# An attention kernel with scaled fp16 weight halves: other steps for the scales' transposes and for loading and splitting one weight, a later low part, another load priority

## The chip, the cores and the metric

The kernel runs on one core of one Trainium2 chip. The core has five engines with instruction queues of their own: PE (TensorE, matmuls into PSUM), DVE (VectorE), ACT (ScalarE), POOL (GpSimd) and SP (SyncE, which here issues all DMAs). Each queue is worked off in order; engines wait for one another by semaphores. The metric is the device time of one execution in microseconds (us), as the median of several runs. A difference under about 0.5% can't be told from no change.

## The reference

Two layers of attention (A) and gated MLP (B) alternate, A B A B, over x of 2048 rows by 640, with the same weights in both layers. Cut to what matters:

```python
def _A_ref(x, wq, wk, wv, wo, beta):        # H = 32 heads of Dh = 20; N = 4 segments of L = 512
    q, k, v = heads(x @ wq), heads(x @ wk), heads(x @ wv)
    for s in range(N):
        logits = einsum("bhqd,bhkd->bhqk", qs, ks) * scale + mask
        a_dot = einsum("bhqk,bhkd->bhqd", softmax(logits), vs)
        a_mem = einsum("bhld,bhde->bhle", phi(qs), M) / (phi(qs) . z + 1e-6)
        outs.append(g * a_mem + (1 - g) * a_dot)
        M, z = M + phi(ks)^T vs, z + sum(phi(ks))
    return concat(outs) @ wo

def _B_ref(x, w_in, w_sp, b_sp, w_out):
    z = gelu(x @ w_in); z1, z2 = halves(z); z2 = layernorm(z2)
    return (z1 * (w_sp @ z2 + b_sp)) @ w_out

x = x + _A_ref(layernorm(x), ...);  x = x + _B_ref(layernorm(x), ...)     # twice
```

## The kernel before, in words

Every matmul operand is kept as two fp16 parts, high and low, whose sum has nearly fp32 precision; a product of two such operands is three fp16 products. A weight is first scaled by a power of two. ACT then writes its high part (`split_scaled`, L81), and DVE subtracts to get the low part (L82). The scales come from the largest entry: DVE reduces the weight's pieces (`other_scales`, L268), PE transposes the row maxima (`pow2_parts`, L60, tile `wtp`), DVE takes the maximum and writes a small diagonal (L62, L64, `wmx` and `wdg`), PE spreads it over all partitions (L67, `wbc`), and DVE makes the power of two of it and its inverse (L69 to L74, `pw` and `iv`).

A layer has three phases: 1a (attention, class `Attention`), 1b (`phase1b`, the rest of the output projection and the first MLP product) and 2 (`phase2`). Phase 1a goes by steps t = -16 to 164, with 16 pairs of heads in each of 4 segments, 64 pairs in all; five steps make a group that serves two pairs. In a step PE does score products for the maxima (`by_queries`, into PSUM tile `mp`, reduced by DVE to `mxs`, L1310 and L1313) and for the exponentials (`by_keys`, into `es`; ACT writes their exponentials `P`, L1287). Once in a group (`maxes`) PE transposes the maxima (`mtp`), ACT and DVE write them in two parts (`mr`, L1333 and L1335), and four DMAs put them beside the keys. `cast` splits P into `PH` (ACT, L1322) and `PL` (POOL, or DVE for the last pair's second head, L1324), `pvs` multiplies them with the values (`pv`), and `combine` normalises the result on DVE (L1364 to L1374 with a `TENSOR_REDUCE` at L1371) or with POOL's help. Only one `pv` tile exists, so the next pair's products wait until `combine` has read it.

Between these products PE does dense ones: the projections of q and k (`unit`, `qps` and `kps`), of values (`value`, `vps`) and of the output (`project`, `yps`). These share two PSUM buffers. `out` of a key unit ends with ACT's exponential of `kps` (L1137) and DVE's `relu` (L1142), after which the buffer is free. The memory part has `read` (`num`, drained by `gm`, L1188) and `update` (`mup`, drained by `mst`, L1209). The tiles `num`, `mup`, `mtp`, `wtp` and `wbc` all have the tag "ms" and share a **single PSUM buffer**: each waits until the one ahead has been drained.

In the first layer weights have to be made as well. `background` does this between the steps: pieces of all four remaining weights are loaded and reduced from step 5 on, then come the scales' transposes (steps 39 and 40), then the rows of w_o are loaded into five buffers of their own (steps 45.5 to 47.5) and split (steps 48 to 53), and then w_in's second half, `wi1`, is loaded and split two pieces behind (from step 57 on, ten pieces). In the second layer all parts are only loaded.

PE's order is that of the program (`manual_schedule`). On the other engines a scheduler sets the order from priorities and a model of the times: `high_priority(offset=n)` lets instructions go ahead by n, and `issue_after(e)` keeps instructions of the block behind e on e's engine, without a wait. `behind(engine)` does the latter for the step's own exponentials (ACT) or maxima (DVE). `post(k, f)` runs f k steps later.

Of the kernel before, what the change touches and what calls it, by code (L numbers as in the profile page):

```python
# [8 lines left out]
F32 = mybir.dt.float32  # L9
# [5 lines left out]
ALU = mybir.AluOpType  # L15
# [3 lines left out]
S, D, H, DH, NSEG = 2048, 640, 32, 20, 4  # L19
L = S // NSEG  # L20
NT = S // 128
KD = D // 128
F, FH = 1728, 864
FHH = FH // 2
# [10 lines left out]
HP2 = 300  # L35
# [226 lines left out]
def other_scales(g, place, pool, psum, tag):  # L262

    nc = g.nc
    raw = []

    def largest():
        nc.vector.tensor_reduce(*raw.pop(0), AX.X, ALU.max, apply_absolute_value=True)  # L268

    for i, w in enumerate((g.wo, *g.wi, g.wu)):  # L270
        width = D if w.cols == D else w.cols // 2
        j = 0
        for k in range(w.nk):
            n = min(128, w.dram.shape[0] - 128 * k)
            for c in range(0, w.cols, width):
                t = place(width)[:n, :width]
                nc.sync.dma_start(t, w.dram[k * 128:k * 128 + n, w.c0 + c:w.c0 + c + width])
                raw.append((g.wap[:n, i, j:j + 1], t))
                if len(raw) > 2:
                    largest()  # L280
                yield True
                j += 1
    while raw:
        largest()
        yield True
    nc.vector.tensor_reduce(g.wam[:, 3:7], g.wap, AX.X, ALU.max)
    yield False
    parts = pow2_parts(g, pool, psum, tag, g.wam, 3, 4)
    next(parts)
    yield False  # L290
    next(parts)
    nc.vector.tensor_scalar(g.yw, g.pw[:, 0:1], g.pw[:, 3:4], 2.0 ** -19, ALU.mult, ALU.mult)
    nc.vector.tensor_scalar(g.sc[:, 8:10], g.pw[:, 4:6], 2.0 ** -24, None, ALU.mult)
# [44 lines left out]
def phase1b(g, o_d, x, x1_d, z1_d, zh, zl):  # L338

    nc, tc = g.nc, g.tc  # L340
    with ExitStack() as ctx:
# [14 lines left out]
        def load(t):  # L356
            if t < NWO:
                x1 = pe2.tile([128, D], F32, tag="x1", name="x1")
                g.loaded[t] = nc.sync.dma_start(x1, x1_d[t])
                return (x1,)  # L360
            xt = px2.tile([128, D], F32, tag="xt", name="xt")
            with tc.issue_after(g.loaded[ORDER[ORDER.index(t) - 1]].ins):
                g.loaded[t] = nc.sync.dma_start(xt, x[t])
            o = px1.tile([128, 2, KD, 128], F16, tag="o", name="o")
            d = o_d[t // 4][(t % 4) * 128:(t % 4 + 1) * 128]
            nc.sync.dma_start(o.rearrange("p i k c -> p (i k) c"), d.rearrange("p i c -> p (i c)"), transpose=True)
            return xt, o[:, 0], o[:, 1]
# [78 lines left out]
        def z1_half(t, zp):  # L446
            z1 = p2.tile([128, FH], F32, tag="z1", name="z1")
            nc.scalar.activation(z1.rearrange("p (n c) -> p n c", n=2), zp[:, :, :FHH], AF.Gelu_apprx_tanh, scale=g.zi[0])  # L448
            nc.sync.dma_start(z1_d[t], z1)

        with tc.high_priority(offset=HP2):
            a = load(0)
            xn = attn_out(0, *a)
            a = load(ORDER[1])
            th = xn_t(*xn)
        for i, t in enumerate(ORDER):
# [6 lines left out]
            if i + 2 < NT:  # L463
                a = load(ORDER[i + 2])
# [449 lines left out]
DVE, ACT = mybir.EngineType.DVE, mybir.EngineType.Activation  # L914


class Attention:
# [68 lines left out]
    def place(self, width):  # L986

        i = self.turn
        self.turn = (i + 1) % (3 if width == D else 4)
        if i < 2:  # L990
            return self.bg.tile([128, D], F32, tag="bg", name="wst")
        if i == 2:
            self.spare = self.pad.tile([128, 2 * FHH], F32, tag="pad", name="wst")
            return self.spare
        return self.spare[:, FHH:]
# [320 lines left out]
    def cast(self, n, h):  # L1316

        nc = self.nc
        P = self.pair(n)
        PH = self.pl3.tile([128, 1280], F16, tag="PH", name="PH")  # L1320
        PL = self.pl2.tile([128, 1280], F16, tag="PL", name="PL")
        nc.scalar.copy(PH, P[:, h])  # L1322
        for c in (slice(0, 640), slice(640, 1280))[::-1 if n % 2 and h else 1]:
            (nc.gpsimd if h == 0 or n < self.N - self.TAIL else nc.vector).tensor_tensor(PL[:, c], P[:, h, c], PH[:, c], ALU.subtract)  # L1324
        self.P[n, h] = (PH, PL)

    def maxes(self, d):
# [69 lines left out]
    def run(self, nseg=NSEG):  # L1397
# [51 lines left out]
        for s in range(nseg):  # L1449
# [4 lines left out]
            for c in seq:  # L1454
                beg = G * s - LEAD + span * acc / tot
                if c == "v":
                    t, w = next(vt), V
# [3 lines left out]
                    it = self.value(t)  # L1461
                    assert s == 0 or beg > G * s + 3, (s, t, beg)
                elif c == "p":
                    t, w = next(pt), Y
                    ev.append((beg - 3, 1, t))
                    it = self.project(t)
                    assert beg - 3 > G * (t // 4 + 1) + 6, (s, t, beg)
                else:
                    m, w = int(c), U
                    if m == 0 and s == nseg - 1:  # L1470
                        continue
                    it = self.unit(s + (m == 0), m)
# [17 lines left out]
        def background():  # L1490

            g = self.g
            made = g.wo.made
            yield 5
            if not made:
                for i, _ in enumerate(other_scales(g, self.place, self.pl1, self.pm, "ms")):
                    yield 5 + i
            yield 45
            yield 45.5
            for j, (w, width) in enumerate(((g.wo, D), (g.wi[1], FHH))):  # L1500
                w.tiles(g.top[j])
                if made:
                    it = w.load(self.bg, width, "bg")
                    times = [46 + 8 * j + 1.4 * i for i in range(99)]
                elif j:
                    it = w.behind(self.place, width, 2)
                    times = [56 + 1.9 * i for i in range(99)]
                else:
                    parts = [g.top[1].tile([128, 2160], F32, tag=f"wi1{x}", name=f"wst{x}3")[:, :3 * D].rearrange("p (k c) -> p k c", c=D) for x in "hl"]
                    rows = iter([parts[k // 3][:, k % 3] for k in range(KD)])  # L1510
                    it = w.behind(lambda _: next(rows), width, KD)
                    times = [46 + i / 2 for i in range(KD)] + [49 + 1.4 * i for i in range(99)]
                for i in range(99):
                    with self.tc.issue_after(self.fetched.ins):
                        if next(it, it) is it:
                            break
                    yield times[i]
            if not made:
                for i, (nm, x, k) in enumerate((nm, x, k) for nm in "qk" for x in range(2) for k in range(KD)):
                    yield 70 + 2 * i  # L1520
                    with self.tc.issue_after(self.fetched.ins):
                        self.nc.sync.dma_start(g.wqk[nm + "hl"[x]][:, k], g.w[nm][x][:, k])

        for _ in early():
            pass
        streams = [[next(it), i, it] for i, it in enumerate((fills(), background(), dense(), reads()))]

        def until(t):
# [8 lines left out]
        for t in range(-LEAD, END):  # L1537
            self.now = t
            d, i = divmod(t + self.LF + 5 + self.DM, 5)
            if i in (0, 2) and 0 <= 2 * d < N:  # L1540
                self.fetch(2 * d + i // 2)
            d, i = divmod(t - 7, 5)
            if i in (0, 2) and 0 <= 2 * d < N:
                p = 2 * d + i // 2
# [6 lines left out]
            d, i = divmod(t + self.DM, 5)  # L1551
# [5 lines left out]
            for d, i, o in PVS:  # L1557
                if t % 5 == i % 5 and 0 <= 2 * (t // 5 - i // 5) < N:
                    p = 2 * (t // 5 - i // 5) + d
# [93 lines left out]
```

## Time and profile before

| | us |
|---|---|
| median of 3 runs | 2235.47 |
| lowest and highest | 2233.04 and 2241.97 |
| the profiled execution | 2232.87 |
| its span, first to last instruction | 2231.2 |
| DVE busy | 1624.2 (73%) |
| POOL busy | 1404.3 (63%) |
| ACT busy | 1252.3 (56%) |

The span is what the profiler saw between the first and the last instruction; all times in views of the trace are counted from its start. Phase 1a of the first layer lies at about 40 to 605 us and that of the second at about 1160 to 1697 us. A view of waits gives the time that an engine stood idle before a line, and the instruction that ended the idle time; when several were waited for it names the last.

### The profile page before, as it was taken

Reading aid. Unit: us, or ns where it says so; the run is one execution under the profiler, and the core shown is the slowest. Engines: PE = TensorE matmul, PEld = TensorE weight load, DVE = VectorE, ACT = ScalarE, POOL = GpSimd, SP = SyncE. Lnnn points to the kernel's source line nnn. Section 1 sums busy time; section 2 is a strip of 40 time slices with the busy share of each in tenths; the row PEclk is TensorE's granted clock in tenths of the full one; section 3 lists DMA queues with packets and bytes.
Section 4 is the critical chain, followed back from the end, with each engine's and each line's share of the span. In section 5 each row is a group of like instructions: output and inputs, shape, how many; then the busy total and the mean of one; then the engine's idle time right before and its main releaser. Section 6 shows DMA issues by size and latency. Waiting matters only on the chain.

```text
span 2231.2 us, 53044 instructions
## 1 busy us (share of the span) xinstructions
PE 2092.0 (94%) x21322; PEld 1264.7 (57%) x21322; DVE 1624.2 (73%) x2889; ACT 1252.3 (56%) x1641; POOL 1404.3 (63%) x1172
## 2 busy tenths in 40 slices
PE   6898788999899999999998999989999999999999
PEld 3554555666555555555554556656675555555555
DVE  8788778788677758888746787787875765676563
ACT  4587688788644433333325887878884433333331
POOL 3387888888645446466513888988895533564660
PEclk9999899999999999999999999999999999999999
DMA  6665556444676686676455356552456345877752
GB/s 185 157 177 141 157 150 188 109 120 126 166 195 188 180 260 191 155 189 175 132 170 129 98 128 166 127 129 75 125 137 152 98 123 175 216 181 177 166 150 83
DMA packets 537703, 342.79 MB, mean 154 GB/s; under 512 B 411600, under 2 KB 463312, under 8 KB 537456
## 3 DMA queue, kind: packets, MB, share of 16 engines
q1 hardware_dynamic: 537456, 339.39, 56.8%
q8 instruction: 167, 2.74, 0.5%
q14 instruction: 80, 0.66, 0.1%
HBM read 159.18 MB, written 92.55 MB: 113 GB/s over the span
## 4 chain that ended last, share of the span: by engine, by line
PE 67%; DVE 14%; ACT 7%; DMA 5%; issue 4%; POOL 2%; SPq 1%; DVEq 0%; ACTq 0%; POOLq 0%
PE zp L412 12%; PE ga L669 12%; PE cyp L705 7%; PE pv L1353 4%; PE qps L1110 3%; PE mp L1249 3%; PE gb L669 3%; PE vps L1051 3%; PE yps L1083 3%; PE gc L669 3%; PE gd L669 3%; DVE mxs L1313 3%; PE kps L1110 2%; PE es L1249 2%; ACT PH L1322 2%
## 5 line engine op out<-in xcount | busy, mean ns | idle before, releaser
L1324 POOL TENSOR_TENSOR PL<-P,PH 128x640 f16<-128x640 f32 x384 | 539.4, 1433 | 91.8 <-PE pv L1353 74.2
L1313 DVE TENSOR_REDUCE mxs<-mp 128x2 f32<-128x1024 f32 (+2 forms) x384 | 320.6, 862 | 135.3 <-PE mp L1240 133.7
L1287 ACT ACTIVATE P<-es,sc 128x1024 f32<-128x1024 f32 (+1 forms) x256 | 271.3, 1060 | 97.0 <-PE es L1240 92.3
L639 POOL TENSOR_TENSOR ts<-ts,wt 128x512 f32<-128x512 f32 x196 | 281.8, 1449 | 11.0
L412 PEld LDWEIGHTS <-th 128*128 128x128 f16 x1920 | 188.0, 98 | 169.3 <-issue 6.6
L1322 ACT CAST PH<-P 128x1280 f16<-128x1280 f32 x192 | 239.6, 1248 | 2.5 <-PE pv L1353 1.0
L669 PEld LDWEIGHTS <-wts 128*128 128x128 f16 x1536 | 150.7, 98 | 134.6 <-issue 6.7
L669 PE MATMUL ga<-zh,wts 128*128 128x432 f16 x768 | 212.0, 348 | 3.9 <-ACT u L736 3.9
L308 POOL TENSOR_TENSOR lnrs<-lnve,mhalf 128x1 f32<-128x1 f32 x96 | 59.7, 629 | 230.0 <-DVE lnve L307 223.7
L1324 POOL TENSOR_TENSOR PL<-Pb,PH 128x640 f16<-128x640 f32 x124 | 176.8, 1454 | 19.8 <-PE pv L1353 18.6
L412 PE MATMUL zp<-wi,th 128*128 128x432 f16 x960 | 181.2, 346 | 3.6 <-ACT z L448 3.6
L1051 PE MATMUL vps<-wvh,xt 128*128 128x320 f16 x640 | 155.5, 309 | 30.3 <-DVE relu L1142 22.1
L639 POOL TENSOR_TENSOR ts<-wt,wt 128x512 f32<-128x512 f16 x28 | 34.4, 1230 | 227.7 <-DMA wt<-wn 227.7
L669 PEld LDWEIGHTS <-wt 128*128 128x128 f16 x1152 | 112.7, 98 | 96.5
L1353 PE MATMUL pv<-vs,PH 128*128 128x41 f16 x2560 | 159.5, 183 | 8.2 <-DVE gm L1374 5.9
L705 PE MATMUL cyp<-wuh,ut 128*128 128x320 f16 (+1 forms) x896 | 163.6, 299 | 2.6 <-DMA ut<-un 1.8
L705 PEld LDWEIGHTS <-ut 128*128 128x128 f16 (+1 forms) x1344 | 131.1, 98 | 57.4 <-DMA ut<-un 3.9
L1249 PEld LDWEIGHTS <-qk 64*128 64x128 f16 (+1 forms) x2048 | 77.6, 94 | 149.4 <-issue 130.9
L1353 PE MATMUL pv<-vs,PL 128*128 128x41 f16 x2560 | 157.2, 182 | 2.2 <-POOL PL L1324 2.2
L412 PE MATMUL zp<-wi1h,th 128*128 128x432 f16 x640 | 149.8, 349 | 1.9 <-DMA th<-xnhl 1.9
L1353 PEld LDWEIGHTS <-PH 128*128 128x128 f16 x2560 | 139.4, 96 | 15.8 <-issue 5.9
L523 DVE SCALAR_TENSOR_TENSOR wn<-wr,wsc,wn 128x512 f16<-128x512 f32 x126 | 92.2, 770 | 75.5 <-ACT wn L522 75.4
(224 smaller groups left out, 5283.3 us busy)
## 6 DMA issues: line engine op xcount, KB each, us to landing
qk<-st SPq DMA_DIRECT2D x256, 120.0 KB
wr<-in_B_w_sp_dram SPq DMA_DIRECT2D x60, 512.0 KB
z<-z SPq DMA_DIRECT2D x32, 432.0 KB
cz<-z SPq DMA_DIRECT2D x32, 432.0 KB
xt<-in_A_x_dram SPq DMA_DIRECT2D x32, 320.0 KB
st<-qhl SPq DMA_DIRECT2D x40, 256.0 KB
st<-khl SPq DMA_DIRECT2D x40, 256.0 KB
x<-x SPq DMA_DIRECT2D x32, 320.0 KB
```

The source lines that it names most:

```text
L412: nc.tensor.matmul(zp[:, n, :FHH], a[:, k, :], b[:, k, c:c + FHH], start=(k == 0 and j == 0), stop=(k == KD - 1 and j == 2))
L639: nc.gpsimd.tensor_tensor(t, a, t if b == "t" else get(b), ALU.add if op == "+" else ALU.subtract)
L669: nc.tensor.matmul(ps, w[:, a, k % 4, :], z[:, k, j, :], start=start and k == 0 and i == 0, stop=k == NP - 1 and i == 2, skip_group_check= ...
L705: nc.tensor.matmul(yp[:, n, :320], a[:kn[k], k, :], b[:kn[k], k, n * 320:(n + 1) * 320], start=(k == 0 and j == 0), stop=(k == KO - 1 and ...
L1051: nc.tensor.matmul(ps, a[:, k, c], b[:, k, n * 320:(n + 1) * 320], start=(i == 0), stop=(i == 14))
L1110: nc.tensor.matmul(ps, a[:, k, c], b[:, k, :], start=(i == 0), stop=(i == 14))
L1249: nc.tensor.matmul(out[:, h, o:o + w], a[r, ac], b[r, bc], start=o == 0, stop=False, skip_group_check=True)
L1287: g.exp = nc.scalar.activation(P, E, AF.Exp, scale=g.esc)
L1313: e = nc.vector.tensor_reduce(mx[:, :, n, j], mp[:, :, o:o + w], AX.X, ALU.max)
L1322: nc.scalar.copy(PH, P[:, h])
L1324: (nc.gpsimd if h == 0 or n < self.N - self.TAIL else nc.vector).tensor_tensor(PL[:, c], P[:, h, c], PH[:, c], ALU.subtract)
L1353: nc.tensor.matmul(pv[:, i, h, :41], x[:, c:c + 128], v[:, j, h0 + h, :], start=(j == 0 and x is PH), stop=(j == i and x is PL), skip_grou ...
```

## The change

There are four edits.

1. `background`, first layer: the scales' transposes go from step 39 to step 41, and the second part (the spreading matmul and the powers of two) from step 40 to step 45. The five row loads of w_o go from steps 45.5 to 47.5 to steps 42 to 44, between the two parts. The splits go from steps 48 to 53.2 to steps 47 to 52.6.
2. All loads and splits of `background` are put behind the step's exponentials on ACT.
3. `cast`: the low part that DVE makes for the last pair is posted two steps later, behind that step's combination.
4. `phase1b`: the load of the first row gets a priority offset of 900 in place of 300.

```diff
-        with tc.high_priority(offset=HP2):
-            a = load(0)
+        with tc.high_priority(offset=3 * HP2):
+            a = load(0)
+        with tc.high_priority(offset=HP2):
             xn = attn_out(0, *a)
...
+        def low(engine):
+            for c in (slice(0, 640), slice(640, 1280))[::-1 if n % 2 and h else 1]:
+                engine.tensor_tensor(PL[:, c], P[:, h, c], PH[:, c], ALU.subtract)
+
+        if h == 0 or n < self.N - self.TAIL:
+            low(nc.gpsimd)
+        else:
+            self.post(2, lambda: low(nc.vector))
...
-                for i, _ in enumerate(other_scales(g, self.place, self.pl1, self.pm, "ms")):
+                scales = other_scales(g, self.place, self.pl1, self.pm, "ms")
+                for i, more in enumerate(scales):
+                    if not more:
+                        break
                     yield 5 + i
+                yield 41
+                next(scales)
...
+            def steps(it, times):
+                for t in times:
+                    with self.tc.issue_after(self.fetched.ins), self.behind(ACT):
+                        if next(it, it) is it:
+                            break
+                    yield t
...
+                it = g.wo.behind(lambda _: next(rows), D, KD)
+                yield 42
+                yield from steps(it, [42.5, 43, 43.5, 44, 45])
+                next(scales, None)
+                yield 47
+                yield from steps(it, [48.4 + 1.4 * i for i in range(99)])
+                g.wi[1].tiles(g.top[1])
+                yield from steps(g.wi[1].behind(self.place, FHH, 2), [56 + 1.9 * i for i in range(99)])
```

The first place is the transpose of the scales in the first layer. On PE it stood before the change behind a step's score products and ahead of a query projection:

```order
L1240 LDWEIGHTS stepk
L1240 MATMUL es<-eye,stepk 128x64
L60 MATMUL wtp<-ident,wam 4x128
L1110 LDWEIGHTS wqh
L1110 MATMUL qps<-xt_302,wqh 128x512
```

Now it stands behind a pair's value products, ahead of the last seven products of the key projection (line numbers from 449 on are shifted):

```order
L1361 LDWEIGHTS PL
L1361 MATMUL pv<-vs_297,PL 128x41
L60 MATMUL wtp<-ident,wam 4x128
L1111 LDWEIGHTS wkh
L1111 MATMUL kps<-xt_302,wkh 128x512
```

The transpose has moved two steps on, past a `num`. On DVE the two operations that follow it stood ahead of `relu`, and the powers of two right behind `gm`:

```order
L1209 TENSOR_TENSOR mst_305<-mup,bmask 128x168
L306 BN_AGGR lnmv<-lnst 128x2
L307 TENSOR_SCALAR lnve<-lnmv 128x1
L62 TENSOR_REDUCE wmx<-wtp 4x1
L64 TENSOR_SCALAR wdg<-ident,wmx 4x4
L1142 SCALAR_TENSOR_TENSOR relu<-kps,relu 128x512
L1313 TENSOR_REDUCE mxs_304<-mp 128x2
L1148 SCALAR_TENSOR_TENSOR phl<-relu,sc,phl 128x512
L1184 SCALAR_TENSOR_TENSOR den<-num,sc,gate 128x24
L1187 RECIPROCAL den<-den 128x24
L1188 TENSOR_TENSOR gm<-num,den 128x4x120
L69 COPY pw<-wbc 128x4
```

Now the same engine reaches `wmx` only after `gm` and three more operations:

```order
L1189 TENSOR_TENSOR gm<-num,den 128x4x120
L1033 TENSOR_SCALAR xt<-xt,lnmv,lnrs 128x640
L1372 TENSOR_TENSOR rs<-pv,iomg 128x8
L1129 SCALAR_TENSOR_TENSOR qhl<-qps,qhl 128x512
L62 TENSOR_REDUCE wmx<-wtp 4x1
L1373 RECIPROCAL rs<-rs 128x8
L64 TENSOR_SCALAR wdg<-ident,wmx 4x4
L1385 TENSOR_TENSOR ab<-pv,rs 128x328
L1141 SCALAR_TENSOR_TENSOR phq<-qps,relu 128x512
L1314 TENSOR_REDUCE mxs_303<-mp 128x2
```

The pair `wmx`, `wdg` has moved behind `gm`, and `relu` no longer has them ahead of it. The second place is the splitting of w_o's rows on ACT (`woh`). Before the change the five stood together, the first of them ahead of the key unit's exponential:

```order
L1287 ACTIVATE P<-es,sc 128x2x512
L81 ACTIVATE woh<-wsth_4007,iv 128x640
L320 CAST xnhl<-xt 128x640
L1322 CAST PH<-P 128x1280
L1056 ACTIVATE vs_297<-vps 128x16x20
L1389 CAST ohl<-gm 128x640
L1137 ACTIVATE kps<-kps,sc 128x512
L81 ACTIVATE woh<-wsth_4007,iv 128x640 x2
L81 ACTIVATE woh<-wstl_4008,iv 128x640
L1147 ACTIVATE phl<-relu,sc 128x512
L81 ACTIVATE woh<-wstl_4008,iv 128x640
```

Now none stands in that stretch; the first comes a group later, behind two exponentials and ahead of ACT's half of `mr`:

```order
L1288 ACTIVATE P<-es,sc 128x2x256
L1288 ACTIVATE Pb<-es,sc 128x2x256
L81 ACTIVATE woh<-wsth_3705,iv 128x640
L1341 ACTIVATE mr<-mtp 16x128
L1323 CAST PH<-P 128x1280
L320 CAST xnhl<-xt 128x640
L1057 ACTIVATE vs_297<-vps 128x16x20
L1288 ACTIVATE Pb<-es,sc 128x2x512
L81 ACTIVATE woh<-wsth_3705,iv 128x640
```

The splits have spread, each behind an exponential; those of `wi1` have moved in the same way, one or two places back. The third place is the end of phase 1a in the first layer, on DVE. Before, the last low part stood ahead of the combination's reduction:

```order
L1364 TENSOR_TENSOR rs<-pv,iomg 128x8
L1365 RECIPROCAL rs<-rs 128x8
L1324 TENSOR_TENSOR PL<-Pb,PH 128x640 x2
L1371 TENSOR_REDUCE pv<-pv 128x160
L1089 SCALAR_TENSOR_TENSOR xt<-yps,sc,xt 128x320
L1373 TENSOR_TENSOR pv<-pv,rs 128x4x2x20
```

Now it stands behind the reduction, and still ahead of the combination's other two operations:

```order
L1372 TENSOR_TENSOR rs<-pv,iomg 128x8
L1373 RECIPROCAL rs<-rs 128x8
L1379 TENSOR_REDUCE pv<-pv 128x160
L1327 TENSOR_TENSOR PL<-Pb,PH 128x640 x2
L1090 SCALAR_TENSOR_TENSOR xt<-yps,sc,xt 128x320
L1381 TENSOR_TENSOR pv<-pv,rs 128x4x2x20
```

One operation has changed places with it. In the second layer it already stood so, and no instruction of any engine changes its place there. The load of the first row of phase 1b stands at the same place in SP's queue before and after, in both layers.

More of the change, by code (lines that the diff above doesn't have):

```diff
@@ L1322, in cast @@
         nc.scalar.copy(PH, P[:, h])
-        for c in (slice(0, 640), slice(640, 1280))[::-1 if n % 2 and h else 1]:
-            (nc.gpsimd if h == 0 or n < self.N - self.TAIL else nc.vector).tensor_tensor(PL[:, c], P[:, h, c], PH[:, c], ALU.subtract)
+        def low(engine):
[5 more added lines that the diff above has]
+            self.post(2, lambda: low(nc.vector))
         self.P[n, h] = (PH, PL)
@@ L1495, in background @@
             if not made:
-                for i, _ in enumerate(other_scales(g, self.place, self.pl1, self.pm, "ms")):
+                scales = other_scales(g, self.place, self.pl1, self.pm, "ms")
+                for i, more in enumerate(scales):
+                    if not more:
+                        break
                     yield 5 + i
[L1498 to L1514, printed above, removed]
@@ L1515, in background @@
+                yield 41
[3 more added lines that the diff above has]
+                    with self.tc.issue_after(self.fetched.ins), self.behind(ACT):
                         if next(it, it) is it:
                             break
-                    yield times[i]
+                    yield t
+            g.wo.tiles(g.top[0])
+            if made:
+                yield 45.5
+                yield from steps(g.wo.load(self.bg, D, "bg"), [46 + 1.4 * i for i in range(99)])
+                g.wi[1].tiles(g.top[1])
+                yield from steps(g.wi[1].load(self.bg, FHH, "bg"), [54 + 1.4 * i for i in range(99)])
+            else:
+                parts = [g.top[1].tile([128, 2160], F32, tag=f"wi1{x}", name=f"wst{x}3")[:, :3 * D].rearrange("p (k c) -> p k c", c=D) for x in "hl"]
+                rows = iter([parts[k // 3][:, k % 3] for k in range(KD)])
+                it = g.wo.behind(lambda _: next(rows), D, KD)
[4 more added lines that the diff above has]
+                yield from steps(it, [48.4 + 1.4 * i for i in range(99)])
+                g.wi[1].tiles(g.top[1])
+                yield from steps(g.wi[1].behind(self.place, FHH, 2), [56 + 1.9 * i for i in range(99)])
```

## The prediction

> **What bounds the kernel now.** The page comes first:
>
> ```profile
> span 2231.2 us, 53044 instructions
> PE 2092.0 (94%) x21322; PEld 1264.7 (57%) x21322; DVE 1624.2 (73%) x2889; ACT 1252.3 (56%) x1641; POOL 1404.3 (63%) x1172
> ```
>
> PE is busy nearly throughout and its order is fixed, so what the change can win is time in which PE stands still; what it adds beside PE costs nothing until PE waits for it. The edits move instructions in the first layer only, which gives a control: the second layer runs the same PE program in phase 1a without scales and splits. So the second view is a table of windows of both layers, cut at the start of ACT's `mr` (L1333), which comes once in a group. The first row goes from the 9th `mr` of a layer to the 10th, the next two are one group each, the fourth covers five; four rows are of the first layer, four of the second.
>
> ```profile
> core 0: us, PE busy (x) PEld busy (x) DVE busy (x) ACT busy (x) POOL busy (x), PEclk, DMA share, GB/s
> 197.17:222.50 25.33, 17.71 (x241) 11.11 (x239) 19.20 (x45) 15.37 (x20) 16.12 (x15) 0.93 0.33 89
> 222.50:247.25 24.75, 15.91 (x235) 10.28 (x233) 15.02 (x30) 18.11 (x26) 17.84 (x16) 0.79 0.71 184
> 247.25:266.04 18.79, 17.59 (x258) 12.72 (x255) 16.26 (x26) 11.81 (x16) 17.34 (x15) 0.91 0.40 113
> 266.04:352.10 86.06, 74.86 (x1151) 48.04 (x1150) 67.26 (x117) 70.17 (x90) 72.41 (x67) 1.00 0.58 158
> 1313.33:1332.22 18.89, 16.60 (x248) 10.35 (x241) 16.05 (x30) 15.46 (x21) 16.37 (x15) 1.00 0.46 112
> 1332.22:1349.24 17.02, 14.29 (x228) 9.69 (x221) 14.90 (x30) 14.43 (x20) 16.24 (x16) 0.90 0.90 214
> 1349.24:1368.46 19.22, 17.76 (x258) 12.58 (x255) 11.70 (x23) 11.81 (x15) 16.16 (x16) 0.91 0.69 167
> 1368.46:1444.81 76.35, 73.88 (x1151) 47.41 (x1150) 55.40 (x105) 65.04 (x80) 69.73 (x66) 1.00 0.53 132
> ```
>
> The first layer takes longer by 25.33 - 18.89 = 6.4, by 24.75 - 17.02 = 7.7, by -0.4 and by 86.06 - 76.35 = 9.7 us: 23.4 us in all. That is the cost of making weights in this stretch, and a ceiling for the change. Third, PE's waits over these windows, first layer, then second:
>
> ```profile
> PE vps L1051 <- DVE relu L1142: 8.8, 1, 8.8
> PE es L1249 <- ACT P L1287: 3.9, 5, 1.6
> PE wbc L67 <- DVE gm L1188: 3.5, 1, 3.5
> PE es L1249 <- ACT Pb L1287: 1.8, 2, 1.4
> ...
> PE vps L1051 <- DVE relu L1142: 2.7, 1, 2.7
> PE es L1249 <- ACT P L1287: 1.2, 2, 1.0
> ```
>
> The extra time is mostly named here: one wait of 8.8 us against 2.7, one of 3.5 us for the scales' second matmul, and 5.7 us for exponentials against 1.2.
>
> **The scales' transposes (first window).** Two waits belong to them, the 3.5 us above and this one:
>
> ```profile
> 207.13 0.27 PE L60 MATMUL wtp<-ident,wam 128*4 128x128 f32 x1 [2.70 <-DVE lnmv L306]
> 207.75 0.72 DVE L64 TENSOR_SCALAR wdg<-ident,wmx 4x4 f32<-4x4 f32 x1
> ```
>
> Both are waits for the one "ms" buffer: `wtp` needs `mup` drained (`mst` stands just ahead of the named `lnmv` on DVE), `wbc` needs `num` drained by `gm`. Their removal brings the window to the control's 18.89, but `wtp` comes back between `gm` and `mtp`. The control and the stretch behind the old `wbc` price that:
>
> ```profile
> 1328.50 0.65 DVE L1188 TENSOR_TENSOR gm<-num,den 128x480 f32<-128x480 f32 x1
> 1329.45 0.39 PE L1331 MATMUL mtp<-ident,mxs 128*16 128x128 f32 x2
> ...
> 219.06 0.38 PE L1110 MATMUL kps<-xt,wkh 128*128 128x512 f16 x1
> 221.38 0.39 PE L1331 MATMUL mtp<-ident,mxs 128*16 128x128 f32 x2
> ```
>
> In the control `gm` ends at 1329.15 and `mtp` follows at 1329.45, with the seven `kps` products and a step's scores done ahead. With `wtp` placed ahead of these, they wait for `gm` too: 0.27 us for `wtp`, then 221.38 - 219.06 = 2.3 us until `mtp`, so 1329.15 + 2.6 = 1331.75, which is **2.3 us late**. DVE's `wmx` comes after three operations and is drained in that time. Bounds: 0.3 us (only `wtp` itself), and 3.3 us (`wmx` and `wdg`, about 1.0 us, also delay `ab` behind them, for which `pv` waits). I take 2.3, since the order on PE forces it. Term: 6.4 - 2.3 = **4.1 us** gained (3.1 to 6.1).
>
> **The loads of w_o and their first split (second window).** ACT, in order of time:
>
> ```profile
> 227.82 1.11 ACT L1287 ACTIVATE P<-es,sc 128x1024 f32<-128x1024 f32 x1 [0.69 <-PE es L1240]
> 233.06 0.83 ACT L81 ACTIVATE woh<-wsth,iv 128x640 f16<-128x640 f32 x1 [4.13 <-DMA wsth<-in_A_wo_dram]
> 233.79 0.71 ACT L320 CAST xnhl<-xt 128x640 f16<-128x640 f32 x1
> 236.51 0.66 ACT L1137 ACTIVATE kps<-kps,sc 128x512 f32<-128x512 f32 x1
> ```
>
> The first split waited 4.13 us for its row, and everything behind it on ACT waited as well: `kps`, then `relu` on DVE, then PE's `vps`, 8.8 us. Now no `woh` stands there, and the rows are loaded a group ahead of their use. What is late next is the same chain without the load; the control shows it as the 2.7 us. New in this window are `wbc`, whose buffer was drained several steps before, and seven small DVE operations behind it:
>
> ```profile
> 215.72 0.16 DVE L69 COPY pw<-wbc 128x4 f32<-128x4 f32 x1 [0.55 <-PE wbc L67]
> 216.58 0.17 DVE L74 TENSOR_SCALAR iv<-iv 128x4 f32<-128x4 f32 x1
> ```
>
> From the first to the end of the last they took 1.0 us, and DVE is busy 14.90 of 17.02 us in the control, so I count it whole: 17.02 + 1.0 = 18.0. The five row loads are the same number on the same queue; they are hidden where the next use is three steps off, and would cost up to the old 4.1 us if they held up the key rows. Term: **6.7 us** (7.7 if DVE hides the small operations, 4.1 if only the wait for the row goes).
>
> After a gap of this kind PE's clock falls, in both layers:
>
> ```profile
> 238.00:243.00 5.00, 5.00 (x44) 2.60 (x43) 3.41 (x5) 4.83 (x6) 2.10 (x3) 0.52 0.96 229
> 1341.00:1346.00 5.00, 5.00 (x72) 3.06 (x72) 4.43 (x8) 3.13 (x4) 5.00 (x4) 0.66 1.11 297
> ```
>
> The granted clock was 0.52 behind the 8.8 us and 0.66 behind the 2.7 us; the control's 17.02 holds the latter, and so does the term. If a gap of 2.7 us didn't lower the clock, the term would grow by up to 5 x (1 - 0.66) = 1.7 us. The Trainium skill speaks for that: "TensorE: Matmul & The Clock Gate", Part 1, has the clock halved after an idle window of about 3.4 us. The trace doesn't bear it out, as the row of 0.66 stands behind a shorter gap.
>
> **The splits (third and fourth window).** ACT's and DVE's share of a split, and what the `wi1` splits waited for:
>
> ```profile
> L81 ACT ACTIVATE woh<-wsth,iv x3: 819/822/827, 233.1 to 237.8; 128x640 f16<-128x640 f32 x3
> L82 DVE SCALAR_TENSOR_TENSOR wol<-wsth,iv,woh x3: 1634/1782/1846, 249.8 to 259.6; 128x640 f16<-128x640 f32 x3
> L82 DVE SCALAR_TENSOR_TENSOR wi1l<-wst,iv,wi1h x10: 705/1191/1817, 283.7 to 345.6; 128x432 f16<-128x432 f32 x10
> ACT wi1h L81 <- DMA wst<-in_B_w_in_dram: 7.4, 5, 3.2
> ```
>
> In the third window DVE had the three low parts of w_o in the row and a fourth behind them, and has four now; ACT gets up to four `woh` at 0.82 us into 11.81 busy of 18.79, each behind an exponential, and hides them. I take the control's 19.22: **0.4 us lost** (none to 2.2, where a fifth low part of 1.78 us falls into it). In the fourth window ten splits of `wi1` stood ahead of exponentials and waited 7.4 us for rows; now the exponentials go first, and PE's waits for them should fall to the control's: 5.7 - 1.2 = **4.5 us**. The low parts on DVE stay, ten at 1.2 us; so do PE's waits for maxima. Bounds: 0 (the delays come back through DVE) and 9.7 (the control).
>
> **The last low part and the first row: nothing.** DVE and PE at the end of phase 1a:
>
> ```profile
> PE pv L1353 <- DVE gm L1374: 2.9, 1, 2.9
> ...
> 596.38 3.11 DVE L1324 TENSOR_TENSOR PL<-Pb,PH 128x640 f16<-128x640 f32 x2
> 599.41 0.49 DVE L1371 TENSOR_REDUCE pv<-pv 128x160 f32<-128x320 f32 x1
> ```
>
> PE waits for `gm`, the end of the combination, and the low part still stands ahead of that; only the reduction of 0.49 us goes past it. So 0, within half a microsecond. The row's load keeps its place in SP's queue: 0.
>
> **Sum.** 4.1 + 6.7 - 0.4 + 4.5 = 14.9 us gained. Bounds: 3.1 + 4.1 - 2.2 + 0 = 5.0 and 6.1 + 7.7 + 0 + 9.7 = 23.5, the ceiling. Nothing later can absorb it, as far as the rows show: PE goes on in its fixed order, with the other engines in step. The span of 2231.2 lies in an execution of 2232.87; this becomes 2218.0. The median of the three runs is 2.6 higher, at 2235.47, and the forecast is on it: 2220.5.
>
> **The rivals.** *The waits re-form*: `wtp` waits for `gm`, the `kps` chain stays long, the splits only change whose turn it is. For it speaks that DVE and POOL are busy 16 of the control's 18.89 us. It gives the lower bound, 2235.5 - 5.0 = 2230.5, within 0.5%. *All goes*: the control's time, 2235.5 - 23.4 = 2212; against it stand ten low parts on DVE. *The clock stays up* after the shorter gap: 2220.5 - 1.7 = 2218.8. *Slower*: the splits now stand ahead of `mr` on ACT and DVE, once in a group. `mr` drains the "ms" buffer and feeds the key rows; each time 0.8 + 1.8 = 2.6 us late twice for w_o and about 1.8 us four times for `wi1`, 12.4 us, decisive only if PE reaches the next user of the buffer with no slack. Then the first two terms' 10.8 us are outweighed with the third's loss: 2237.5, and twice the price would be 2250. Against it stands PE's only wait for `mr` in the first layer's four windows:
>
> ```profile
> PE mup L1203 <- DVE mr L1335: 0.3, 1, 0.3
> ```
>
> It is 0.3 us, although DVE's low parts stood among the same operations before. *That the change doesn't do what it says* holds for the last two edits already.
>
> **How the numbers follow.** Forecast 0.62 (2216 to 2224), the clock stays up 0.05, all goes 0.06, the waits re-form 0.23 (2224 to 2231), slower 0.04. The range 2213 to 2230 takes in the bounds and leaves out the slower case, half of "all goes" and the end of "re-form". 0.5% is 11.2 us, about what a measurement can tell from no change: faster than that are the forecast, the clock and "all goes", 0.73; slower half of its case, 0.02; the same 0.25.
>
> **What would show it.** In the new profile `wbc` has no wait, `wtp` waits for `gm`, the 8.8 us of `vps` is about 3, no `woh` waits for a row, and the four windows are near 21.2, 18.0, 19.2 and 81.6 us, with phase 2 and the second layer as before. I am wrong if `mtp` or `mup` waits for `mr` behind a split, if the fourth window stays at 86, or if time won by 352 is lost again by the end of the layer.

## The result and the profile after

| us | before | changed | ratio, 95% interval |
|---|---|---|---|
| first chip, median of 6 runs each | 2234.03 (2228.73 to 2241.97) | 2221.93 (2220.00 to 2223.77) | 0.9947, 0.9929 to 0.9964 |
| second chip, medians of 11 and 6 runs | 2235.80 (2227.12 to 2242.54) | 2219.85 (2217.23 to 2221.53) | 0.9927, 0.9909 to 0.9946 |
| profiled execution, its span | 2231.2 | 2219.7 (in a run of 2221.43) | |

The change gains 12.1 us on the first chip. The page of the changed kernel, span and engines, shows the same PE work in less time:

```profile
span 2219.7 us, 53060 instructions
PE 2089.0 (94%) x21322; PEld 1263.9 (57%) x21322; DVE 1620.1 (73%) x2889; ACT 1252.7 (56%) x1641; POOL 1402.1 (63%) x1172
```

The table of windows, cut at the same `mr` as before (length, busy time of PE, PEld, DVE, ACT and POOL, granted clock, DMA share, GB/s); four rows of the first layer, four of the second:

```profile
200.50:222.02 21.52, 16.21 (x239) 10.13 (x237) 17.47 (x38) 15.23 (x21) 17.57 (x16) 1.00 0.68 167
222.02:244.98 22.96, 18.00 (x242) 11.63 (x239) 17.06 (x38) 15.44 (x22) 17.07 (x16) 0.78 0.60 148
244.98:262.35 17.37, 16.05 (x267) 11.96 (x267) 15.05 (x26) 14.69 (x20) 17.03 (x15) 1.00 0.46 127
262.35:344.80 82.45, 73.73 (x1144) 47.32 (x1137) 67.85 (x115) 70.10 (x90) 73.22 (x68) 1.00 0.58 162
1301.54:1320.43 18.89, 16.62 (x248) 10.37 (x243) 16.06 (x30) 15.47 (x20) 16.36 (x15) 1.00 0.48 124
1320.43:1337.41 16.98, 14.25 (x228) 9.67 (x221) 14.87 (x30) 14.55 (x21) 16.20 (x16) 0.90 0.86 223
1337.41:1356.19 18.78, 17.58 (x258) 12.68 (x255) 11.76 (x23) 11.81 (x15) 16.22 (x16) 0.91 0.71 161
1356.19:1432.56 76.37, 73.88 (x1151) 47.40 (x1150) 55.39 (x105) 65.08 (x80) 69.76 (x66) 1.00 0.53 132
```

| window of the first layer | before | forecast | after | gain forecast | gain measured |
|---|---|---|---|---|---|
| first | 25.33 | 21.2 | 21.52 | 4.1 | 3.8 |
| second | 24.75 | 18.0 | 22.96 | 6.7 | 1.8 |
| third | 18.79 | 19.2 | 17.37 | -0.4 | 1.4 |
| fourth | 86.06 | 81.6 | 82.45 | 4.5 | 3.6 |
| sum | 154.93 | 140.0 | 144.30 | 14.9 | 10.6 |

The second layer hardly moved: its windows sum to 131.02 us, and to 131.48 before. Of the span's 11.5 us the four windows hold 10.6. The first window starts 3.3 us later than before (the last section has the cause), and what lies behind the fourth took 1874.9 us, against 1879.1 before. Two more executions of the changed kernel, e5 and e9 below, had 1878.4 and 1874.1 there, so those 4.2 us are within what one kernel shows.

The second window holds the miss. PE's waits of the changed kernel, the first three rows in the first window, the next in the second, the others in the fourth (line, what ended the wait: total us, times, longest):

```profile
PE wtp L60 <- DVE gm L1189: 2.3, 1, 2.3
PE num L1176 <- DVE lnmv L306: 1.5, 1, 1.5
PE pv L1361 <- DVE ab L1385: 1.5, 1, 1.5
...
PE vps L1052 <- DVE relu L1143: 5.0, 1, 5.0
...
PE mup L1204 <- DVE mr L1343: 1.1, 1, 1.1
PE es L1250 <- ACT P L1288: 1.0, 2, 0.7
...
PE es L1250 <- ACT Pb L1288: 0.4, 1, 0.4
```

`wbc` has no wait any more, `wtp` waits 2.3 us for `gm`, and the exponentials keep PE for 1.4 us in place of 5.7. But `vps` still waits 5.0 us, where the forecast had 2.7. The timelines of ACT and then DVE in the changed kernel, second window (start, duration, engine, line, operation, and in brackets the idle time ahead of it), show why:

```profile
229.40 0.72 ACT L320 CAST xnhl<-xt 128x640 f16<-128x640 f32 x1 [0.95 <-DVE xt L1033]
230.03 1.25 ACT L1323 CAST PH<-P 128x1280 f16<-128x1280 f32 x1
231.19 0.44 ACT L1057 ACTIVATE vs<-vps 128x320 f16<-128x320 f32 x1
231.53 0.71 ACT L1397 CAST ohl<-gm 128x640 f16<-128x640 f32 x1
232.13 0.66 ACT L1138 ACTIVATE kps<-kps,sc 128x512 f32<-128x512 f32 x1
...
228.14 1.23 DVE L1033 TENSOR_SCALAR xt<-xt,lnmv,lnrs 128x640 f32<-128x640 f32 x1
229.29 0.68 DVE L1129 SCALAR_TENSOR_TENSOR khl<-kps,khl 128x512 f16<-128x512 f32 x1
...
232.83 0.69 DVE L1143 SCALAR_TENSOR_TENSOR relu<-kps,relu 128x512 f32<-128x512 f32 x1 [2.62 <-ACT kps L1138]
```

The same place in the control, the second layer of the kernel before, ACT and then DVE:

```profile
1337.95 1.26 ACT L1322 CAST PH<-P 128x1280 f16<-128x1280 f32 x1
1339.11 0.66 ACT L1137 ACTIVATE kps<-kps,sc 128x512 f32<-128x512 f32 x1
...
1337.35 0.68 DVE L1128 SCALAR_TENSOR_TENSOR khl<-kps,khl 128x512 f16<-128x512 f32 x1
1337.95 0.32 DVE L1209 TENSOR_TENSOR mst<-mup,bmask 128x168 f32<-128x168 f32 x1
1338.19 0.97 DVE L1032 TENSOR_SCALAR xt<-xt,lnmv,lnrs 128x640 f32<-128x640 f32 x1
```

In the control DVE does `khl` ahead of `xt`, and ACT's exponential of `kps` follows its cast at once. In the first layer `xt` goes first; ACT waits 0.95 us for it and does `xnhl`, `vs` and `ohl` ahead of `kps` as well, and `relu` and PE's `vps` wait for that. No transfer is in this chain.

### The profile page after: what moved, and what is told of

It is laid out like the page before. It is cut to its first block, busy times and chain, and to the rows that moved or that the text cites. A ratio compares the mean times of both kernels' runs of the same rounds, so it can differ in the third digit from the quotient of the medians.

```text
span 2219.7 us, 53060 instructions
## 1 busy us (share of the span) xinstructions
PE 2089.0 (94%) x21322; PEld 1263.9 (57%) x21322; DVE 1620.1 (73%) x2889; ACT 1252.7 (56%) x1641; POOL 1402.1 (63%) x1172
## 4 chain that ended last, share of the span: by engine, by line
PE 68%; DVE 13%; ACT 8%; DMA 5%; issue 4%; POOL 2%; SPq 1%; ACTq 0%; DVEq 0%; POOLq 0%
PE zp L412 12%; PE ga L670 12%; PE cyp L706 7%; PE pv L1361 4%; PE vps L1052 4%; PE qps L1111 3%; PE mp L1250 3%; PE gb L670 3%; PE yps L1084 3%; PE gc L670 3%; PE gd L670 3%; DVE mxs L1314 3%; PE kps L1111 2%; ACT PH L1323 2%; PE es L1250 2%
```

## The experiments

Windows below are those of the first layer, cut in the same way. A single time has before's own spread, 13 to 15 us in the runs above, so these runs are read by windows and waits. All kernels but e3 and e4 start from the changed kernel; those two start from the kernel before.

**e1, e10, e11: the key unit first.** One kernel, run three times, which gives the key unit's two operations a higher priority:

```diff
+            with self.tc.high_priority(offset=100 if not q and not g.wo.made and self.now in (42, 43, 44) else 0):
                 nc.vector.scalar_tensor_tensor(hl[:, 1], ps, QS, hl[:, 0], ALU.mult, ALU.subtract)
...
+            with self.tc.high_priority(offset=100 if not q and not g.wo.made and self.now in (42, 43, 44) else 0):
                 nc.scalar.activation(ps, ps, AF.Exp, scale=g.rq if q else g.rk)
```

> The changed kernel, with the key unit's low part (DVE) and exponential (ACT) at steps 42 to 44 of the first layer given priority, so that they stand ahead of the normalisation xt and of xnhl, vs and ohl, as they do in the second layer. Theory A (the second window stayed long because its key unit's exponential stands behind four other ACT operations, and the clock falls behind the long gap): PE's wait for relu falls from 5.0 to about 2.5 us and the second window from 23.0 to about 18.0 us. Rival B (the row loads of w_o, now beside the key rows, or the scales' small operations hold it up): the wait changes by under 1 us and the window stays above 22 us. Rival C (the order matters but the clock does not): the wait falls by 2.5 us and the window by no more than that, to 20.5 us. The other windows stay at 21.5, 17.4 and 82.5 us.

> The first experiment's kernel once more, to tell what the second window holds beside the wait: it had 21.40 us with a wait of 2.5 us at a granted clock of 0.84, and the kernel with late scales 18.70 with 2.7 us at 0.91. Clock theory: the wait stays at 2.5 us, and the second window follows the granted clock of the execution, about 21.4 at 0.84 and 1 us or more shorter if the clock falls for less time. Rival (the spreading matmul and the small operations behind it, or work that slid over the cut): 21.4 whatever the clock.

> As the run before it: by the clock theory the first two windows sum to 42.9 us at a clock of 0.84 in the second, and to less at a higher one, down to about 41; by the rival 42.9 whatever the clock.

In all three the wait of `vps` is 2.5 us, half of the changed kernel's, so the order is the cause of that half. The second window missed what e1 expected of it, 18.0 us by theory A and at most 20.5 by rival C: it took 21.40. The times were 2219.87, 2216.41 and 2212.85 us. The first two windows sum to 42.90, 42.51 and 42.64 us, against 44.48 in the changed kernel and 44.02 in both its repeats (e5 and e9): 1.4 us by the medians, less than the 2.5 us of the wait; where the other 1.1 went is open. The clock doesn't make this difference: weighted by the windows' lengths it was 0.92 in e1 and e11 as in the repeats, which leaves 1.1 to 1.4 us. How far executions scatter is shown by e7 below, whose edit lies elsewhere: its two windows sum to 45.57 us, with the clock below 1.00 in both. First to third window of e10, and then the second of e1 and that of e11:

```profile
198.84:221.67 22.83, 17.51 (x239) 10.45 (x237) 18.24 (x39) 15.22 (x21) 17.77 (x16) 0.93 0.66 159
221.67:241.35 19.68, 15.11 (x242) 10.39 (x240) 16.12 (x35) 15.37 (x21) 17.08 (x16) 1.00 0.76 171
241.35:260.65 19.30, 17.69 (x268) 12.87 (x268) 15.80 (x29) 14.70 (x19) 16.30 (x15) 0.91 0.40 113
```

```profile
221.63:243.03 21.40, 17.91 (x242) 11.56 (x240) 16.11 (x36) 15.48 (x21) 17.27 (x17) 0.84 0.65 158
```

```profile
220.64:241.78 21.14, 17.99 (x242) 11.63 (x240) 15.92 (x36) 15.49 (x21) 17.27 (x17) 0.84 0.66 160
```

With the same wait and 242 matmuls, the second window is 19.68 us at a clock of 1.00 and 21.14 to 21.40 at 0.84: the clock is worth 1.5 to 1.7 us of that window, and the fixed 21.4 of the rival is out. But e10 was no faster over the first two windows: its clock fell in the first (22.83 at 0.93, against 21.50 at 1.00 in e1 and e11) and in the third (19.30 at 0.91, against 17.72 and 17.68 at 1.00). The fall had only moved, so the 41 us that the clock theory allowed was not seen. The second layer shows the same: its second window ran at 1.00 in e6 and e7 and took 16.96 and 16.73 us, against 16.93 to 17.22 at 0.90 in the other executions; in e6 and e7 the window ahead of it held a fall instead (19.58 and 19.56 us at 0.91).

**e2: the transposes at a late step.** The transposes go behind the row loads again, past the stretch in question:

```diff
-                yield 41
-                next(scales)
...
+                next(scales)
+                yield 46
                 next(scales, None)
                 yield 47
```

> The changed kernel, with the scales' first transpose at step 45 and the spreading matmul at step 46, both behind the loads of w_o's rows. Theory A (the transpose costs 2.3 us in the first window because it waits for gm in the one ms buffer, ahead of the key products): no wait for gm, first window 18.9 to 19.2 us in place of 21.5. Rival B (the first window is bound by DVE and POOL, both over 16 us busy, and the wait only changes its place): first window above 20.5 us. At steps 45 and 46 the buffer has been drained, so neither matmul waits there; the second window grows by under 1 us.

Time 2217.31 us. First and second window, then PE's three longest waits in them:

```profile
200.84:221.81 20.97, 17.25 (x253) 10.64 (x251) 16.92 (x36) 15.12 (x21) 17.02 (x15) 1.00 0.68 169
221.81:240.51 18.70, 15.64 (x236) 10.64 (x229) 16.51 (x38) 15.39 (x22) 17.85 (x18) 0.91 0.92 184
```

```profile
PE vps L1052 <- DVE relu L1143: 2.7, 1, 2.7
PE num L1176 <- DVE lnmv L306: 1.5, 1, 1.5
PE pv L1361 <- DVE ab L1385: 1.5, 1, 1.5
```

`wtp` waits for nothing now, and `khl` also comes ahead of `xt`, so this run undoes both. By the first window alone, 20.97 us, theory A's 18.9 to 19.2 was missed and rival B's sign came true. But the window holds 253 matmuls where the changed kernel has 239, and the second shrank by 3.8 us or more where a growth under 1 us was expected. So the cost shows mostly in the next window, and the two are read together, which was decided after the result. They sum to 39.67 us (489 matmuls), against 44.0 of the changed kernel (its repeats, 481) and 42.6 of e1 (the median, 481): the order of the key unit is worth 1.4 us, the place of the transposes 3.0. Against e10, the one execution of e1's kernel with the same clock of 0.96 over both windows, it is 2.8. The control has 35.91 still, 3.8 less. Of these, 1.5 is `pv` waiting for `ab`; this row stands in the first layer's first window of the kernel before too, and not in the control's. In e2 DVE starts this `ab` 3.0 us after the maximum (`mxs`) ahead of it, with a reduction of a weight's piece (`wap`, 0.80 us), `mr` and another maximum between them; in the control it starts 1.15 us after, ahead of `mr`. That this order makes the wait is argued from these rows; no run changed it.

**e3 and e4: one half each.** e3 puts the scales' steps alone into the kernel before, e4 the place behind the exponentials alone:

```diff
+                yield 41
+                next(scales)
             yield 45
+            if not made:
+                next(scales, None)
             yield 45.5
```

```diff
-                    with self.tc.issue_after(self.fetched.ins):
+                    with self.tc.issue_after(self.fetched.ins), self.behind(ACT):
```

> The kernel before, with only the scales' two parts moved to steps 41 and 45; loads and splits of w_o stay where they were, and nothing is put behind exponentials. Theory A (the terms add up, one part of the change for each window): first window 21.5 us as in the changed kernel, second near the 24.8 us of before with the 8.8 us wait of vps still there, fourth near 86 us. Rival B (the second window's long wait comes from the late scales as well): vps waits less than 6 us.

> The kernel before, with only the loads and splits put behind the step's exponentials on ACT; the scales stay at steps 39 and 40, the loads at 45.5. Theory A (the fourth window's gain comes from splits of wi1 no longer standing ahead of exponentials): first window 25.3 us as before, fourth near 82.5 us as in the changed kernel. For the second window: if putting the splits behind exponentials is what takes woh out of the key unit's way, it is near 23 us even without the earlier loads; if the earlier loads are what matters, it stays at 24 to 25 us with ACT waiting for a row.

| us | first | second | third | fourth | sum | time |
|---|---|---|---|---|---|---|
| before | 25.33 | 24.75 | 18.79 | 86.06 | 154.93 | 2232.87 |
| e3, scales alone | 22.88 | 24.90 | 17.61 | 86.87 | 152.26 | 2227.62 |
| e4, behind alone | 26.78 | 20.97 | 18.08 | 83.30 | 149.13 | 2229.32 |
| changed | 21.52 | 22.96 | 17.37 | 82.45 | 144.30 | 2221.43 |

PE's waits in the second window, of e3 and then of e4:

```profile
PE vps L1051 <- DVE relu L1142: 4.9, 1, 4.9
PE es L1249 <- ACT P L1287: 2.7, 1, 2.7
```

```profile
PE vps L1051 <- DVE relu L1142: 4.9, 1, 4.9
```

Either half takes the wait of `vps` from 8.8 to 4.9 us without the early loads of w_o's rows, so those loads earned little of it; no run has both halves without them. In e3, where theory A expected the 8.8 us to stay, rival B's sign came true, though the window stayed as long: the splits then stand ahead of an exponential (2.7 us). Over the first two windows both halves have 47.8 us, against 50.1 before. The first window's gain is the scales': 22.88 us in e3, and 22.85 and 22.83 in e7 and e10, which have their place too, against 25.33 before, all at a clock of 0.93. That is 2.5 us at the same clock; the changed kernel's 21.52 has 1.00. The fourth window's gain is the place behind the exponentials (83.30 against 86.87).

**e5 and e6: the changed kernel again, and without the place behind the exponentials.**

```diff
-                    with self.tc.issue_after(self.fetched.ins), self.behind(ACT):
+                    with self.tc.issue_after(self.fetched.ins):
```

> The changed kernel once more, unaltered. In the profiles so far the third, fourth and fifth group of the first layer took 15.2 us in some and 16.7 us in others, although every engine's instructions stand in the same order there. Theory A (behind PE's gaps of 2 to 5 us the granted clock falls or not, and for longer or shorter, from one execution to the next): some of these groups change between 15.2 and 16.7, and the second window, 23.0 us with 10 us below full clock, comes out different by over 0.5 us with the same 5.0 us wait of vps. Rival B (the fall follows from the code): second window 22.8 to 23.2 us and the same groups slow as in the first profile of this kernel.

> The changed kernel without the second edit: loads and splits are no longer put behind the step's exponentials; the new steps stay. ACT then has the five woh together, about one group earlier than in the changed kernel, ahead of an exponential. Theory A (the exponentials' priority is what the fourth window gains from, and the spread of woh helps the second and third): fourth window 85 to 87 us in place of 82.5, second 23 to 25 us. Rival B (the earlier steps alone bring it): fourth window under 83.5 us, second 23.0.

e5 repeats the 5.0 us of `vps`, with windows of 21.51, 22.51, 17.38 and 82.44 us. That decides neither way: the second window moved by 0.45 us, short of theory A's 0.5 and out of rival B's 22.8 to 23.2, and the same early groups were slow as in the first profile. e9 below, the same kernel, settles the groups: there two of them took 15.2 us that had 16.5 to 16.8 in both, and a third 16.78 in place of 15.2. e6 has 21.52, 25.29, 19.83 and 86.32. In e6's second window, and then in its fourth, PE waits for exponentials again:

```profile
PE es L1250 <- ACT P L1288: 3.0, 1, 3.0
...
PE es L1250 <- ACT P L1288: 3.9, 4, 1.5
PE es L1250 <- ACT Pb L1288: 2.3, 2, 1.9
```

Edit 2 is thus worth 9.1 us of these windows beside the others, of which the third's 2.5 holds a clock of 0.89 against 1.00. The single times don't show it: 2224.95 and 2226.21 us, with mean granted clocks of 0.990 and 0.992 over the execution. Behind the fourth window e6 took 1871.0 us and e5 1878.4; all thirteen executions lie at 1868.6 to 1879.1 there, so one pair can't tell whether any of the 9.1 is lost again.

**e7: the last low part behind the whole combination.**

```diff
-            self.post(2, lambda: low(nc.vector))
+            def last():
+                with self.tc.issue_after(self.combined.ins):
+                    low(nc.vector)
+
+            self.post(2, last)
...
-            nc.vector.tensor_tensor(o, a, o, ALU.add)
+            self.combined = nc.vector.tensor_tensor(o, a, o, ALU.add)
```

> The changed kernel, with the last low part on DVE held behind the last operation of the combination, gm, in both layers, which is what the third edit meant to do. Theory A (the edit changed nothing because the low part still stands ahead of gm, for which PE waits 2.6 us in the first layer and 2.3 in the second): these two waits go, PE waits for the low part itself later, and each layer's end of phase 1a is shorter by 0.5 to 2.5 us. Rival B (the low part is then what is late, by as much): PE's waits for PL grow by the same 2 to 3 us, and nothing is won. The windows of before stay as in the changed kernel.

DVE at the end of phase 1a of the first layer, of the changed kernel and then of e7:

```profile
588.57 2.77 DVE L1327 TENSOR_TENSOR PL<-Pb,PH 128x640 f16<-128x640 f32 x2
...
592.40 0.31 DVE L1382 TENSOR_TENSOR gm<-pv,gm 128x160 f32<-128x160 f32 x1
```

```profile
588.58 0.32 DVE L1386 TENSOR_TENSOR gm<-pv,gm 128x160 f32<-128x160 f32 x1
588.82 1.86 DVE L1327 TENSOR_TENSOR PL<-Pb,PH 128x640 f16<-128x640 f32 x2
```

In the changed kernel PE waits 2.6 us for that `gm` (2.9 before); the edit went past the reduction alone, as forecast. In e7 this wait is gone in both layers, with 0.7 us for the low part itself and up to 1.9 us for a transposing DMA (`zp` for `th`) in its place. From the last `mr` to the end, the second layer took 560.9 us in e7 and 562.1 in e8 below, and 563.3 to 566.0 in eleven executions of kernels without this edit (before, changed, e1 to e6, e9 to e11): 1.2 to 2.4 us less than the lowest of them. In the first layer the same stretch, up to the next layer's first `mr`, took 619.1 in e7 and 614.6 in e8, and 617.6 to 622.6 in those eleven, which settles nothing there. The first two windows did not stay as in the changed kernel, although the edit lies at the end of phase 1a: 22.85 and 22.72 us, at clocks of 0.93 and 0.85. Time 2215.51 us.

**e8 and e9: both repairs together, and the changed kernel beside it.** e8 is e2 with e7's edit (and e1's priority, which moves nothing there); e9 is the changed kernel.

> The changed kernel with the scales at steps 45 and 46, the last low part held behind gm, and the key unit's priority of the earlier run, which leaves the order as the late scales alone make it. Theory A (the two gains are in different places and add): first and second window together 39 to 40 us against 44.5 in the changed kernel, no wait of pv for gm in either layer, median 2209 to 2215 us. Rival B (the late scales' gain was a lucky clock, the held low part's a lucky start of phase 1b): the two windows together over 43 us, median 2218 to 2224 us, as the changed kernel.

> The changed kernel unaltered, timed on the same chip for comparison: 2220 to 2225 us median by all theories, second window 22.5 to 23.0 us with a wait of 5.0 us.

On one chip e8 had a median of 2213.66 us (2210.95 to 2214.87, five runs), the changed kernel 2219.85 and the kernel before 2235.80; e8's ratio to before is 0.9898 (0.9879 to 0.9916). e8 beats both: its runs and the changed kernel's (2217.23 to 2221.53) don't overlap, though 6.2 us is less than the 0.5% named at the start. Its first two windows:

```profile
199.19:220.17 20.98, 17.25 (x253) 10.63 (x251) 16.93 (x36) 15.14 (x21) 17.03 (x15) 1.00 0.68 169
220.17:238.88 18.71, 15.63 (x236) 10.70 (x229) 16.53 (x38) 15.51 (x22) 17.86 (x18) 0.91 0.89 184
```

They repeat e2's to 0.01 us, 39.69 in all. Against e9's 44.02 that is 4.3 of the 6.2 us between the medians.

## Why the prediction was right, and the step that failed

The forecast of 2220.5 stands 1.4 us below the measured 2221.93. The way there was less exact: of 14.9 us the windows gave 10.6, and the medians moved by 12.1. Half of the 2.8 us missing was made up by luck: the forecast counts from 2235.47, the median of three runs of before, and six runs have 2234.03. More luck lies in the clock, which was higher in the changed kernel's first and third window than in those of before.

*The scales' transposes* (4.1, measured 3.8). `wbc` lost its wait and `wtp` waits 2.3 us for `gm`, as worked out. At the same clock the window gained 2.5 (e3, e7, e10); the other 1.3 is a fall of the clock that the profile of before had and that of the changed kernel had not. It came in both executions with the old place (before, e4) and in three of nine with the new one, too few to say that the change removes it. e2 shows what the place of the transpose costs over two windows: 3.0 us. Most of it appeared in the second.

*The loads and the first split* (6.7, measured 1.8). **This is the step that failed:** "What is late next is the same chain without the load; the control shows it as the 2.7 us." The load did go, no `woh` waits for a row, but the chain isn't the control's. The order of the first layer has `xt` ahead of `khl`, and with that three more ACT operations ahead of `kps`, which left the wait at 5.0 us; e1 brought it to 2.5. The rows of order quoted with the change already had `xnhl`, `vs` and `ohl` ahead of `kps` in the first layer; I priced the place from the other layer's. Taken over two windows, the forecast had 39.2 us and the changed kernel's repeats 44.0. The runs size the 4.8 us between: 1.4 for this order (e1 against the changed kernel), 0.7 for the transposes above their 2.3 (e2 against e1), and 2.8 in which even e2 stays above the control beyond the 1.0 us booked for the small operations. Of the last, 1.5 is the wait of `pv` for `ab`, which stood in the trace of before and which I had counted as going. On DVE one of the weights' last reductions stands ahead of it (0.80 us, under e2); that it causes the wait wasn't tested, and what the other 1.3 are is open.

*The third window* (-0.4, measured 1.4). The clock decided it, not the splits: 17.4 to 18.1 us where the clock was 1.00 (changed, e1 to e5, e8, e9, e11) and 18.8 to 19.8 at 0.89 to 0.91 (before, e6, e7, e10). The control's 19.22 and the 18.79 of before both held a fall. ACT took its four splits at 14.69 us busy, hidden as forecast.

*The fourth window* (4.5, measured 3.6). The waits for exponentials fell as forecast, and e4 and e6 show that edit 2 did it. It gave back 0.8 us: the wait of `mup` for `mr` went from 0.3 to 1.1 us in the changed kernel and in e4, and is absent in e6. On DVE this `mr` stands right behind a low part of `wi1`, so here the forecast's own sign of being wrong came true. That is the mechanism of the slower rival, at 0.8 us in place of 12.4.

*The last low part and the first row* (0). The first is shown by the trace and by e7: the wait stayed. The second kept its place in the queue and was not tried alone.

Of the rivals, "the waits re-form" was right about `vps` and wrong about its price. "The clock stays up" came true in the second window of e10, where it bought nothing, as the fall stood in the windows beside it; so the 1.7 us that it was priced at is not borne out. Time won by the fourth window was not seen to be lost again.

## What to carry to other kernels

A second pass over the same code is a control for the work only as far as the scheduler put that work in the same order: compare the order of the chain that will be late next, on every engine of it, before taking its wait from there. When an instruction is moved ahead of a wait, judge it over as many windows as its displaced work needs to come back. And an edit that means to go behind a chain has to be held behind its last operation: two steps later in the program moved it past one of three, and an explicit order past all, which with the late transposes made 6.2 us of difference.

## What the runs showed of the hardware

The clock fell at other places in executions of the same order, and after short gaps. The group from the first layer's fourth `mr` to its fifth has the same instructions in all these kernels. In the changed kernel and in e2 it had the same waits of PE too, 1.7 us for `mr` and 0.3 for an exponential; its windows in the one and then in the other:

```profile
119.54:136.11 16.57, 14.42 (x220) 9.27 (x220) 12.72 (x24) 12.98 (x17) 14.02 (x12) 0.90 0.71 199
```

```profile
119.68:134.91 15.23, 13.08 (x220) 8.35 (x220) 12.63 (x24) 12.98 (x18) 14.03 (x12) 1.00 0.78 216
```

e9, an execution of the changed kernel itself, has 15.23 us at 1.00 there, again with these two waits, so neither the order nor the waits decide it. One fall costs 1.3 us here: the clock was 0.50 from 121.5 to 124.5 us, behind the wait of 1.7 us that ended at 121.1. This group and the one ahead of it (16.73 us against 15.22) make 2.9 of the 3.3 us by which the changed kernel reached the first window later than before. The Trainium skill, "TensorE: Matmul & The Clock Gate", Part 1, says that the activity window is free-running, so that the number of slow matmuls at a kernel's start differs from run to run; these rows show the like in the middle of one. The same part of the Trainium skill has the clock halved after an idle window of some 3.4 us. Here it fell with no wait over 2 us in the group, so that figure was no bound. Nor did a gap always bring a fall: with the second layer's 2.5 to 2.7 us wait of `vps` its window had a clock of 0.90 in eleven executions and 1.00 in e6 and e7.

A kernel's spread goes with the falls in large part: among the eleven runs of the kernel before beside e8, the fastest had 2227.12 us at a mean granted clock of 0.992 and the slowest 2242.54 at 0.984, about 1.9 us for each 0.001. The changed kernel's six lay at 0.990 to 0.993, where time and clock go together less closely (2217.23 and 2220.30 us both at 0.993). At 0.990 one run of before had 2231.79 us, and two of the changed kernel 2219.94 and 2221.53: 10 to 12 us, about the windows' gain. By these three runs, the other 4 to 6 of the 16 us between the medians on that chip go with the clock; whether the change makes falls rarer, or those runs met fewer, is open.
